# Inverse stage: the left-over rows of tiles 3 and 4 go through a DRAM stack of their own

## Chip, cores and metric

The kernel runs on one core of one Trainium2 chip. The metric is the device time of one launch in microseconds (us). Before the change it is 672.01 us (median of 3 runs, 671.79 to 672.07).

## What is computed

The input x has 2048 rows of 640 numbers in float32. A spectral layer is added to it and then a bilinear gated layer, each behind a layer norm:

```python
X = rfft2(layernorm(x)) * (w_r + 1j * w_i)
h = x + irfft2(X, s=(2048, 640))
n = layernorm(h)
out = h + ((n @ w_gate) * (n @ w_up)) @ w_down
```

## The kernel before

**Stages.** The transforms are done as matrix products on TensorE (PE). A forward stage turns the 16 tiles of 128 rows into spectra, a middle stage of 16 groups g multiplies by the filter, an inverse stage takes the 16 tiles t back along the 640 axis and the 2048 axis and adds x, and then the gated layer runs over blocks of weights until the end. The change lies in the inverse stage, with the last steps of the middle stage ahead of it.

**The inverse stage.** The middle stage leaves its result in two SBUF tensors: qm holds four main chunks of 128 frequencies for each tile, and qr the left-over frequencies, as a rounded high part (partitions 0 to 63) and a low part (partitions 64 to 127), with one edge frequency kept apart. For each tile, id_mm(t) multiplies the main chunks (matmuls eo<-tab,qm 128x161) and then the left-over rows into the same PSUM pair eo, of which there are two. unfold(t) takes eo through ScalarE (ACT, s), VectorE (DVE, q) and GpSimd (POOL, yt) to a buffer yt; is1_mm(t) multiplies that by the second transform (y<-yt,tab); acc(t) adds the result to x. The loop at the stage's end runs, for step t, unfold(t+2), id_mm(t+3), is1_mm(t), so PE's order is id 0, id 1, id 2, id 3, y 0, id 4, y 1, id 5, y 2 and on.

**Two ways for the left-over rows.** Tiles 0 to 4 are plain: five matmuls eo<-xt,qr of 322 columns with qr as it lies. Tiles 5 to 15 are stacked: high, low and high rows of one quarter lie above each other in 99 partitions, and four matmuls of 162 columns do the work (operand xt or si, 99 partitions). To move rows to other partitions the kernel goes through DRAM. ispread(a, o) writes the rows of some tiles from qr to a DRAM tensor ifar in five DMAs: two of 33 rows, two of 32 rows (L707) and one small one for the edge rows (L710). istack(t, n) reads n tiles back in two DMAs: 66 partitions (L718, high and low) and 33 partitions (L719, high again), each of 4 quarters times n x 128 numbers. Every piece of a row is n x 512 bytes long, and there are 99 x 4 = 396 pieces whatever n is.

**The order around the change.** All these DMAs are issued by one engine, SyncE (SP), in program order, and they share its queue. load_direct issues the first weight load (raw<-in_wlast_dram), then what is in its argument mid, then two more weight loads (raw<-in_wgu_dram), and istack for tiles 9 to 11 comes behind them. In mid stood: write tiles 5 to 8, read tiles 5 to 8, write tiles 9 to 15. istack for tiles 12 to 15 is issued when id_mm(8) is. A read waits on SP until the writes of its own DRAM tensor have landed, and what is behind it on SP waits too. Completion is counted on eight semaphores that SP's DMAs use in turn, so that a DMA also waits for the one eight places ahead of it to have landed. The weights that the two raw loads bring are split by ACT (L657, wdir) and POOL (L658) in the steps after (aside), between the unfold steps.

The stack of tiles 5 to 8 lies in the buffer near (named xt in the profile), the one of tiles 9 to 11 in the home "dC" (named si), and the one of tiles 12 to 15 in near again.

Of the kernel before, what the change touches and what calls it, by code (L numbers as in the profile page):

```python
# [11 lines left out]
F32 = mybir.dt.float32  # L12
F32R = mybir.dt.float32r
# [3 lines left out]
P = 128  # L17
S, D, NF, FF = 2048, 640, 321, 1728
NT = S // P
# [6 lines left out]
RWHERE = ((1, 0), (0, 0), (1, 160), (0, 160))  # L26
RW = (160, 194, 162, 162)
PLAIN, MID = 5, 10
IPLAIN, IFAR = 5, 9
SUMS = 7  # L30
IPARTS = ((5, 4), (9, 3), (12, 4))
AGAIN = {0: (5, 3, "dC"), 1: (8, 2, "qt"), 4: (10, 3, 0), 7: (13, 3, 1)}
NR = 4
AHEAD = 5
# [15 lines left out]
def f32(ap):  # L50
    return ap.bitcast(F32)
# [29 lines left out]
def tile_spectral_glu(ctx: ExitStack, tc: tile.TileContext, x, wre, wim, wgu, wlast, wdown, wdlast,  # L81
                      cc, ci, fmain, frem, imain, irem, mm, out):
    nc = tc.nc
# [4 lines left out]
    far = ctx.enter_context(tc.tile_pool(name="far", bufs=1, space=bass.MemoryType.DRAM))  # L88
# [16 lines left out]
    def pair(tag):  # L105
        return pools["a" if tag == "eo" else "y"].tile([P, 2, 512], F32, tag=tag, name=tag, bufs=2)
# [13 lines left out]
    def mmx(o, l, r, start, stop):  # L120
        nc.tensor.matmul(o, l, r, start=start, stop=stop, skip_group_check=True)  # L121
# [14 lines left out]
    def home(tag, shape, name, dt=F32):  # L136
        return keep.tile(shape, dt, tag=tag, name=name)

    def cut(t, o, *shape):
        v = t[:, o:o + int(np.prod(shape))]  # L140
        names = [f"d{i}" for i in range(len(shape))]
        return v.rearrange(f"p ({' '.join(names)}) -> p {' '.join(names)}", **dict(zip(names[1:], shape[1:])))
# [279 lines left out]
    def parts(ps, main, rest):  # L422
        for k, (b, o, w, l, r) in enumerate(main):
            mmx(ps[b][:, o:o + w], l, r, k < 2, False)
        for k, (b, l, r) in enumerate(rest):
            mmx(ps[b][:, 0:NQ], l, r, False, k >= len(rest) - 2)
# [154 lines left out]
    for g in range(NG - 1):  # L581
# [4 lines left out]
        if g + 3 == NG:  # L586
# [3 lines left out]
            scrap, near = cut(flat, 2258, D), cut(flat, 2258 + D, 4, 4, P)  # L590
# [20 lines left out]
        elif g == 1:  # L611
            rest_low(MID, NG)
            qr = home("qr", [P, 2, NT, P], "qr", F32R)
# [37 lines left out]
    def split_in(key, w, src, raws, engine):  # L651
        W[key] = w
        his, los = [], []
        for i, r in enumerate(raws):
            a, b = 640 * i, 640 * i + 640
            nc.sync.dma_start(r, src[:, a:b])
            his.append(lambda r=r, a=a, b=b: act(w[:, 0, a:b], r, AF.Copy))  # L657
            los.append(lambda r=r, a=a, b=b: engine.tensor_tensor(w[:, 1, a:b], r, f32(w[:, 0, a:b]), op=OP.subtract))  # L658
        return his, los

    def load_direct(blk, raws, engine=nc.gpsimd, mid=()):
        w = home("wA" if blk == 0 else "wB", [P, 3840], "wdir", F32R)
        first = split_in(NC - 1, cut(w, 0, 2, 640), wlast, raws[:1], engine)
        for f in mid:
            f()
        return [first, split_in(NC - 2, cut(w, 1280, 2, 1280), wgu[NC - 2], raws[1:], engine)]
# [30 lines left out]
    PE_, PY, YT, Z = {}, {}, {}, {}  # L697

    SI = {}
    ifar = [(a, far.tile([2, 2, 2, 33, b - a, P], F32, name="ifar")) for a, b in ((IPLAIN, IFAR), (IFAR, NT))]  # L700

    def ispread(a, o):
        ts = slice(a, a + o.shape[4])
        for h in (1, 0):
            for l in range(2):
                r = 64 * l + 31 * h
                nc.sync.dma_start(o[:, h, l, 1 - h:33].rearrange("b r t n -> r b t n"),  # L707
                                  f32(qr[r:r + 32 + h, :, ts]))
        e = f32(qr[0:65:64, 1, ts])
        nc.sync.dma_start(o[:, 0, :, 0].rearrange("b l t n -> l b (t n)"),  # L710
                          bass.AP(tensor=e.tensor, offset=e.offset,
                                  ap=[list(e.ap[0]), [0, 2], [1, P * o.shape[4]]]))

    def istack(t, n):
        o = near[:, :, 0:n] if t != 9 else home("dC", [P, 4, 3, P], "si", F32R)
        a, i = ifar[t >= IFAR]
        src = i[:, :, :, :, t - a:t - a + n].rearrange("b h l r t n -> (l r) (b h) (t n)")
        nc.sync.dma_start(f32(o[0:66]).rearrange("p q t n -> p q (t n)"), src)  # L718
        nc.sync.dma_start(f32(o[66:99]).rearrange("p q t n -> p q (t n)"), src[0:33])  # L719
        for i in range(n):  # L720
            SI[t + i] = o[:, :, i]

    def id_mm(t):
        ps = PE_[t] = pair("eo")
        main = [(b, o, 161, qm[:, c, t], imt[:, c]) for c, (b, o) in enumerate(((0, 0), (1, 0), (0, 161), (1, 161)))]
        if t not in SI:
            parts((ps[:, 0], ps[:, 1]), main,
                  [(b, qr[:, k, t], irt[:, c]) for c, b, k in ((0, 0, 0), (2, 0, 0), (1, 1, 1), (3, 0, 1), (4, 1, 1))])
            return
        parts((ps[:, 0], ps[:, 1]), main, [])  # L730
        for q, (b, h) in enumerate(((0, 0), (0, 1), (1, 0), (1, 1))):
            mmx(ps[:, b, 160 * h:160 * h + 162], SI[t][0:99, q], sirt[0:99, q], False, h == 1)
        if t == 8:
            istack(*IPARTS[2])

    def unfold(t, side, turns=(), extra=()):
        ps = PE_[t]
# [149 lines left out]
    for ts in (range(3), range(3, 6), range(6, 8)):  # L887
        n, t0 = len(ts), ts[-1] + 1
# [10 lines left out]

    tside[NT - 1] = []  # L900
    raw0 = home("dA", [P, 3, D], "raw0")
    jobs = load_direct(0, [raw0[:, i] for i in range(3)], mid=(
        lambda: ispread(*ifar[0]), lambda: istack(*IPARTS[0]), lambda: ispread(*ifar[1])))
    istack(*IPARTS[1])
    for i, (h, l) in enumerate((h, l) for hs, ls in jobs for h, l in zip(hs, ls)):
        aside[2 + i] += [h, l]
    id_mm(0)
    id_mm(1)
    unfold(0, [])
    id_mm(2)  # L910
    unfold(1, [])

# [640 lines left out]
```

## Time and profile before

| what | value |
|---|---|
| runs | 672.01 us (671.79 to 672.07) |
| the profiled execution, time | 672.12 us |
| its span | 670.3 us |
| PE busy | 661.2 us, 3695 matmuls |
| DVE, ACT, POOL busy | 468.7, 321.6, 393.3 us |
| inverse stage, first matmul of id_mm(0) | at 107.16 us |
| first matmul of the gated layer | at 151.5 us |

The span runs from the first to the last instruction of the program, and the time has 1.8 us around it. A matmul in float32 counts twice on PE (x8 in the trace for the four main matmuls of a tile), one in the rounded type fp32r once. Starts are given in us from the span's start. SPq is the queue side of SP; its time is the issue of a DMA, not the transfer.

### The profile page before, as it was taken

Reading aid. Unit: us, or ns where it says so; the run is one execution under the profiler, and the core shown is the slowest. Engines: PE = TensorE matmul, PEld = TensorE weight load, DVE = VectorE, ACT = ScalarE, POOL = GpSimd, SP = SyncE. Lnnn points to the kernel's source line nnn. Section 1 sums busy time; section 2 is a strip of 40 time slices with the busy share of each in tenths; the row PEclk is TensorE's granted clock in tenths of the full one; section 3 lists DMA queues with packets and bytes.
Section 4 is the critical chain, followed back from the end, with each engine's and each line's share of the span. In section 5 each row is a group of like instructions: output and inputs, shape, how many; then the busy total and the mean of one; then the engine's idle time right before and its main releaser. Section 6 shows DMA issues by size and latency. Waiting matters only on the chain.

```text
span 670.3 us, 10240 instructions
## 1 busy us (share of the span) xinstructions
PE 661.2 (99%) x3695; PEld 588.2 (88%) x3695; DVE 468.7 (70%) x952; ACT 321.6 (48%) x622; POOL 393.3 (59%) x377
## 2 busy tenths in 40 slices
PE   7999999999999999999999999999999999999997
PEld 7999988887888888888888899888888888888887
DVE  6969996788767767594857567754757485757644
ACT  6977774585525244453626146634434251624220
POOL 3101124750297977968696445188786869697610
PEclk9999999999999999999999999999999999999999
DMA  8639875502212120042332467212002121212004
GB/s 318 227 113 280 246 245 151 165 2 80 78 40 80 39 79 23 31 106 60 98 79 83 94 133 260 78 42 75 11 36 76 40 79 40 79 40 80 1 0 157
DMA packets 48953, 66.12 MB, mean 99 GB/s; under 512 B 24082, under 2 KB 30670, under 8 KB 48774
## 3 DMA queue, kind: packets, MB, share of 16 engines
q1 hardware_dynamic: 48246, 62.91, 30.4%
q0 software_dynamic: 288, 2.16, 0.8%
q8 instruction: 29, 0.48, 0.3%
q10 hardware_dynamic: 368, 0.39, 0.3%
q14 instruction: 22, 0.18, 0.1%
HBM read 54.61 MB, written 10.84 MB: 98 GB/s over the span
## 4 chain that ended last, share of the span: by engine, by line
PE 94%; ACT 2%; DVE 2%; DMA 1%; issue 0%; DVEq 0%
PE e L121 50%; PE d L121 26%; PE eo L121 4%; PE y L121 2%; PE re L121 2%; PE u L476 2%; PE im L121 2%; PE im L528 2%; PE im L270 2%; PE ir L528 1%; DMA x<-in_x_dram 1%; ACT s L296 1%; ACT fold L212 0%; ACT fold L211 0%; PE y L794 0%; ACT bits L285 0%
## 5 line engine op out<-in xcount | busy, mean ns | idle before, releaser
L121 PE MATMUL e<-xt,wst 128*128 128x512 f32 x864 | 211.1, 390 | 0.0
L121 PEld LDWEIGHTS e<-xt,wst 128*128 128x128 f32 x864 | 160.7, 188 | 31.7
L1073 DVE TENSOR_TENSOR x<-d,x 128x320 f32<-128x320 f32 x280 | 120.3, 482 | 41.2 <-PE d L121 37.1
L121 PE MATMUL d<-wd,ht 128*128 128x320 f32 x832 | 142.1, 309 | 0.0
L121 PEld LDWEIGHTS d<-wd,ht 128*128 128x128 f32 x832 | 129.6, 188 | 5.1
L987 POOL TENSOR_TENSOR wst<-raw,wst 128x1024 fp32r<-128x1024 f32 x23 | 55.5, 2412 | 69.9 <-ACT wst L986 69.9
L121 PE MATMUL e<-t,wst 128*128 128x512 f32 x360 | 94.0, 391 | 0.0
L121 PEld LDWEIGHTS e<-t,wst 128*128 128x128 f32 x360 | 66.7, 188 | 13.0
L121 PE MATMUL d<-wt,ht 128*128 128x320 f32 x360 | 68.9, 309 | 0.0
L1003 POOL TENSOR_TENSOR wst<-raw,wst 128x896 fp32r<-128x896 f32 (+1 forms) x46 | 65.1, 1438 | 0.2 <-ACT wst L998 0.2
L121 PEld LDWEIGHTS d<-wt,ht 128*128 128x128 f32 x360 | 57.3, 188 | 0.8
L1089 ACT ACTIVATE ht<-e 128x512 fp32r<-128x512 f32 x44 | 26.4, 599 | 49.6 <-DVE e L1151 24.0
L998 ACT ACTIVATE wst<-raw 128x896 fp32r<-128x896 f32 (+1 forms) x48 | 30.1, 676 | 30.8 <-POOL raw L992 30.1
L1147 DVE TENSOR_TENSOR e<-e,h 128x512 f32<-128x512 f32 x24 | 16.8, 698 | 39.8 <-ACT wst L998 18.9
L1048 DVE TENSOR_TENSOR x<-d,x 128x320 f32<-128x320 f32 x62 | 27.5, 484 | 22.2 <-PE d L121 22.2
L121 PE MATMUL e<-xt,wdir 128*128 128x512 f32 x180 | 42.2, 392 | 0.0
L679 ACT ACTIVATE wd<-draw 128x320 fp32r<-128x320 f32 (+1 forms) x30 | 15.7, 561 | 55.1 <-POOL draw L689 52.3
L1127 ACT ACTIVATE h<-e 128x512 f32<-128x512 f32 x24 | 14.3, 596 | 56.7 <-PE e L121 56.7
L121 PEld LDWEIGHTS e<-xt,wdir 128*128 128x128 f32 x180 | 33.3, 188 | 7.8 <-ACT xt L804 0.5
L1092 DVE TENSOR_TENSOR ht<-e,ht 128x512 fp32r<-128x512 f32 x54 | 36.9, 685 | 1.6 <-ACT ht L1089 1.3
L1144 ACT ACTIVATE h<-e 128x512 f32<-128x512 f32 x24 | 14.3, 597 | 46.7 <-PE e L121 46.7
L658 POOL TENSOR_TENSOR wd<-draw,wd 128x640 fp32r<-128x640 f32 x8 | 12.5, 1577 | 40.9 <-ACT wd L657 40.9
(236 smaller groups left out, 1188.9 us busy)
## 6 DMA issues: line engine op xcount, KB each, us to landing
raw<-in_wgu_dram SPq DMA_DIRECT2D x24, 640.0 KB
draw<-in_wdown_dram SPq DMA_DIRECT2D x24, 320.0 KB
wts<-in_wre_dram SPq DMA_DIRECT2D x16, 322.0 KB
x<-in_x_dram SPq DMA_DIRECT2D x15, 320.5 KB
out_dram<-x SPq DMA_DIRECT2D x15, 320.0 KB
bits<-in_mm_dram SPq DMA_DIRECT2D x32, 128.0 KB
wts<-in_wim_dram SPq DMA_DIRECT2D x9, 322.0 KB
zfar<-zr SPq DMA_DIRECT2D x32, 80.0 KB
```

The source lines that it names most:

```text
L121: nc.tensor.matmul(o, l, r, start=start, stop=stop, skip_group_check=True)
L528: nc.tensor.matmul(out, y[:, h, a:b], inv(g, h), start=n == 0, stop=n == len(ys) - 1)
L679: act(o[:, 0, a:a + n], src, AF.Copy)
L987: ptt(wa[:, 1], stage[:, 0:1024], f32(wa[:, 0]), op=OP.subtract)
L998: act(ws[:, 0, o:o + b - a], stage[:, a:b], AF.Copy)
L1003: ptt(ws[:, 1, o:o + b - a], stage[:, a:b], f32(ws[:, 0, o:o + b - a]), op=OP.subtract)
L1048: tt(xv, ps[b][:, 0:320], xv, op=OP.add)
L1073: tt(xv, o, xv, op=OP.add)
L1089: act(hop[:, a, 0], src, AF.Copy)
L1092: engine.tensor_tensor(hop[:, a, 1], src, f32(hop[:, a, 0]), op=OP.subtract)
L1127: act(h0, oa, AF.Copy)
L1147: tt(ob, ob, h1, op=OP.add)
```

## The change

Tiles 3 and 4 are stacked as well, with a DRAM tensor of their own. IFAR now lists three ranges of tiles (3 and 4; 5 to 8; 9 to 15), and IPARTS has a read of two tiles ahead of the others. ispread no longer issues its five DMAs at once but returns them as a list, and mid puts them in this order: the five writes of tiles 3 and 4, three of the five writes of tiles 5 to 8, the read of tiles 3 and 4, the other two writes of tiles 5 to 8, the read of tiles 5 to 8, the five writes of tiles 9 to 15. The two weight loads and the read of tiles 9 to 11 follow as before. The new stack lies in the home "dC", which the stack of tiles 9 to 11 takes over when id_mm(4) has read it.

```diff
--- before.py
+++ after.py
@@ -26,9 +26,9 @@
 RWHERE = ((1, 0), (0, 0), (1, 160), (0, 160))
 RW = (160, 194, 162, 162)
 PLAIN, MID = 5, 10
-IPLAIN, IFAR = 5, 9
+IFAR = ((3, 5), (5, 9), (9, NT))
 SUMS = 7
-IPARTS = ((5, 4), (9, 3), (12, 4))
+IPARTS = ((3, 2), (5, 4), (9, 3), (12, 4))
 AGAIN = {0: (5, 3, "dC"), 1: (8, 2, "qt"), 4: (10, 3, 0), 7: (13, 3, 1)}
 NR = 4
 AHEAD = 5
@@ -697,23 +697,26 @@
     PE_, PY, YT, Z = {}, {}, {}, {}
 
     SI = {}
-    ifar = [(a, far.tile([2, 2, 2, 33, b - a, P], F32, name="ifar")) for a, b in ((IPLAIN, IFAR), (IFAR, NT))]
+    ifar = [(a, far.tile([2, 2, 2, 33, b - a, P], F32, name="ifar")) for a, b in IFAR]
 
     def ispread(a, o):
         ts = slice(a, a + o.shape[4])
-        for h in (1, 0):
-            for l in range(2):
-                r = 64 * l + 31 * h
-                nc.sync.dma_start(o[:, h, l, 1 - h:33].rearrange("b r t n -> r b t n"),
-                                  f32(qr[r:r + 32 + h, :, ts]))
-        e = f32(qr[0:65:64, 1, ts])
-        nc.sync.dma_start(o[:, 0, :, 0].rearrange("b l t n -> l b (t n)"),
-                          bass.AP(tensor=e.tensor, offset=e.offset,
-                                  ap=[list(e.ap[0]), [0, 2], [1, P * o.shape[4]]]))
+
+        def rows_of(h, l):
+            r = 64 * l + 31 * h
+            nc.sync.dma_start(o[:, h, l, 1 - h:33].rearrange("b r t n -> r b t n"), f32(qr[r:r + 32 + h, :, ts]))
+
+        def edge_rows():
+            e = f32(qr[0:65:64, 1, ts])
+            nc.sync.dma_start(o[:, 0, :, 0].rearrange("b l t n -> l b (t n)"),
+                              bass.AP(tensor=e.tensor, offset=e.offset,
+                                      ap=[list(e.ap[0]), [0, 2], [1, P * o.shape[4]]]))
+
+        return [lambda h=h, l=l: rows_of(h, l) for h in (1, 0) for l in range(2)] + [edge_rows]
 
     def istack(t, n):
-        o = near[:, :, 0:n] if t != 9 else home("dC", [P, 4, 3, P], "si", F32R)
-        a, i = ifar[t >= IFAR]
+        o = near[:, :, 0:n] if t in (5, 12) else home("dC", [P, 4, n, P], "si", F32R)
+        a, i = [f for f in ifar if f[0] <= t][-1]
         src = i[:, :, :, :, t - a:t - a + n].rearrange("b h l r t n -> (l r) (b h) (t n)")
         nc.sync.dma_start(f32(o[0:66]).rearrange("p q t n -> p q (t n)"), src)
         nc.sync.dma_start(f32(o[66:99]).rearrange("p q t n -> p q (t n)"), src[0:33])
@@ -731,7 +734,7 @@
         for q, (b, h) in enumerate(((0, 0), (0, 1), (1, 0), (1, 1))):
             mmx(ps[:, b, 160 * h:160 * h + 162], SI[t][0:99, q], sirt[0:99, q], False, h == 1)
         if t == 8:
-            istack(*IPARTS[2])
+            istack(*IPARTS[3])
 
     def unfold(t, side, turns=(), extra=()):
         ps = PE_[t]
@@ -899,9 +902,10 @@
 
     tside[NT - 1] = []
     raw0 = home("dA", [P, 3, D], "raw0")
+    first, second, third = (ispread(*f) for f in ifar)
     jobs = load_direct(0, [raw0[:, i] for i in range(3)], mid=(
-        lambda: ispread(*ifar[0]), lambda: istack(*IPARTS[0]), lambda: ispread(*ifar[1])))
-    istack(*IPARTS[1])
+        *first, *second[:3], lambda: istack(*IPARTS[0]), *second[3:], lambda: istack(*IPARTS[1]), *third))
+    istack(*IPARTS[2])
     for i, (h, l) in enumerate((h, l) for hs, ls in jobs for h, l in zip(hs, ls)):
         aside[2 + i] += [h, l]
     id_mm(0)
```

On SP's queue, from the first left-over rows on, stood before (ifar<-qr are writes, xt<-ifar and si<-ifar reads; 512 numbers are four tiles, 896 seven, 384 three):

```order
L707 DMA ifar<-qr 33x2x512 x2
L707 DMA ifar<-qr 32x2x512 x2
L710 DMA ifar<-qr 2x2x512
L718 DMA xt<-ifar 66x4x512
L719 DMA xt<-ifar 33x4x512
L707 DMA ifar<-qr 33x2x896 x2
L707 DMA ifar<-qr 32x2x896 x2
L710 DMA ifar<-qr 2x2x896
L656 DMA raw_1298<-in_wgu_dram 128x640 x2
```

The read of tiles 5 to 8 was the sixth and seventh DMA of this list. The same place now (256 numbers are two tiles; the functions lie some lines further down, so L707, L711, L721 and L722 are the old L707, L710, L718 and L719):

```order
L707 DMA ifar<-qr 33x2x256 x2
L707 DMA ifar<-qr 32x2x256 x2
L711 DMA ifar<-qr 2x2x256
L707 DMA ifar<-qr 33x2x512 x2
L707 DMA ifar<-qr 32x2x512
L721 DMA si<-ifar 66x4x256
L722 DMA si<-ifar 33x4x256
L707 DMA ifar<-qr 32x2x512
L711 DMA ifar<-qr 2x2x512
L721 DMA xt<-ifar 66x4x512
L722 DMA xt<-ifar 33x4x512
L707 DMA ifar<-qr 33x2x896 x2
```

The new read of two tiles is the ninth and tenth DMA, and the read of tiles 5 to 8 has moved from the sixth place to the thirteenth; the remaining writes, the two weight loads and the read of tiles 9 to 11 follow behind it.

On PE, the difference at tiles 3 and 4 (eo<-tab,qm is a tile's main part, y<-yt,tab a second transform; the names in brackets are what the instruction waits for, DMAHW a DMA of SP):

```order
 L121 MATMUL eo<-tab,qm 128x161 x3
-L121 MATMUL eo<-xt,qr 128x322 x5
+L121 MATMUL eo<-xt,si 128x162 [waits DMAHW7_49,DMAHW0_49]
+L121 MATMUL eo<-xt,si 128x162 x3
 L121 MATMUL y<-yt,tab 128x320 [waits DMAHW2_49,Pool_49]
 L121 MATMUL y<-yt,tab 128x320
 L121 MATMUL eo<-tab,qm 128x161 [waits DVE_49,Activation_49]
 L121 MATMUL eo<-tab,qm 128x161 x3
-L121 MATMUL eo<-xt,qr 128x322 x5
+L121 MATMUL eo<-xt,si 128x162 x4
```

In each of the two tiles five matmuls of 322 columns have become four of 162, and the first of tile 3 waits for the two DMAs of the new read. Nothing else has moved on PE, nor on DVE, ACT or POOL.

## The prediction

> **What bounds the kernel now.** I read the page first, then the windows, then PE's timeline around the inverse stage, then SP's. The page gives the span and PE's share, and the clock that PE was granted in 40 slices:
>
> ```profile
> span 670.3 us, 10240 instructions
> PE 661.2 (99%) x3695; PEld 588.2 (88%) x3695; DVE 468.7 (70%) x952; ACT 321.6 (48%) x622; POOL 393.3 (59%) x377
> PEclk9999999999999999999999999999999999999999
> ```
>
> One window from the first tiles of the inverse stage nearly to the end (its length, then PE's busy time):
>
> ```profile
> 107.63:654.00 546.37, 546.37 (x2882) 1.00 0.24 71
> ```
>
> PE has no idle time in these 546.37 us. PE works in order, so a microsecond that PE loses or saves at tile 3 moves everything after it by a microsecond, unless something that doesn't hang on PE comes late. The change touches PE's work here (start, length, what):
>
> ```profile
> 112.79 1.26 PE L121 MATMUL eo<-tab,qm 128*128 128x161 f32 x8
> 113.78 1.01 PE L121 MATMUL eo<-xt,qr 128*128 128x322 f32 x5
> 114.63 1.24 PE L121 MATMUL y<-yt,tab 128*128 128x320 f32 x4
> ...
> 116.70 1.01 PE L121 MATMUL eo<-xt,qr 128*128 128x322 f32 x5
> ...
> 119.62 0.68 PE L121 MATMUL eo<-xt 99*128 99x162 f32 x4
> ```
>
> These are tile 3 (main at 112.79, left-over rows at 113.78), tile 4's left-over rows at 116.70, and at 119.62 the first stacked matmuls, those of tile 5. So PE asks for a stack of tile 5 at 119.62 now, and would ask for one of tile 3 at 113.78. When can the stacks be there? SP's issues, from the first left-over rows on:
>
> ```profile
> 106.76 2.19 SPq L707 DMA_DIRECT2D ifar<-qr  x4
> 109.00 0.58 SPq L710 DMA_DIRECT2D ifar<-qr  x1
> 111.06 0.30 SPq L718 DMA_DIRECT2D xt<-ifar  x1
> 111.41 0.39 SPq L719 DMA_DIRECT2D xt<-ifar  x1
> 111.85 2.18 SPq L707 DMA_DIRECT2D ifar<-qr  x4
> 114.06 0.51 SPq L710 DMA_DIRECT2D ifar<-qr  x1
> 114.61 3.07 SPq L656 DMA_DIRECT2D raw<-in_wgu_dram  x2
> 120.69 0.32 SPq L718 DMA_DIRECT2D si<-ifar  x1
> 121.05 0.39 SPq L719 DMA_DIRECT2D si<-ifar  x1
> 128.20 0.28 SPq L718 DMA_DIRECT2D xt<-ifar  x1
> ```
>
> The writes start at 106.76, when qr is ready, and take until 109.58 to issue. The read of tiles 5 to 8 starts at 111.06, when they have landed, 1.48 us later. It must be there at 119.62, and PE doesn't wait: the round trip through DRAM is hidden behind the five plain tiles, and it is this cover that the change shortens.
>
> **Term 1, the matmuls: 0.66 us less.** The chain of waits merges a tile's main part and left-over rows into one piece:
>
> ```profile
> 115.87 1.84 PE eo L121 x13
> ...
> 118.79 1.51 PE eo L121 x12
> ```
>
> A plain tile (x13, tile 4) costs 1.84 us and a stacked one (x12, tile 5) 1.51. Two tiles save 2 x 0.33 = 0.66 us, all on PE's path.
>
> **Term 2, when the small read is issued.** The five writes of tiles 3 and 4 have as many pieces as those of tiles 5 to 8 had, each half as long, and begin when qr is ready, so I leave their issue at 106.76 to 109.58. Three writes of tiles 5 to 8 come next; at 2.18 / 4 = 0.55 us each they are issued by 111.2. By then the first five have landed (111.06 before, with longer rows). The small read is issued at 111.2.
>
> **Term 3, how long it takes.** No read of two tiles stands alone in the trace. The nearest rows are the read of three tiles, issued at 120.69, and the last one of four, issued at 128.20. The traffic of the DMA engines after them, in slices of 0.15 us from 120.6 and of 0.2 us from 128:
>
> ```profile
> DMA  8662203983252677777877677676421000000000
> GB/s 324 256 273 103 102 34 75 113 72 61 61 102 102 236 266 266 276 266 236 195 143 164 154 215 205 236 256 205 113 51 21 0 0 0 0 0 0 0 0 0
> ```
>
> ```profile
> DMA  0000048924357786868677686776320000000000
> GB/s 0 0 0 0 0 61 102 102 92 102 82 205 276 287 266 164 195 143 195 143 205 215 174 174 143 195 205 154 92 62 20 0 0 0 0 0 0 0 0 0
> ```
>
> The first six slices of the upper pair are the end of the weights. Three tiles are read by 125.25 (31 slices), 4.56 us after the issue, and four by 134.2, 6.0 us after it. Between the last traffic and the release lies more, as the writes show (slices of 0.3 us from 106.6):
>
> ```profile
> GB/s 0 0 0 205 178 123 198 164 198 239 287 185 48 7 0 0 0 7 123 41 150 171 157 266 266 169 193 224 157 159 210 229 239 304 297 364 352 348 309 364
> ```
>
> Their traffic ends in the slice up to 110.8, and SP goes on at 111.06. I add 0.5: 5.05 us for three tiles and 6.5 for four. Going on along that line gives 5.05 - 1.45 = 3.6 for two. But each read has the same 396 pieces, and each begins with a slow microsecond (34 to 113 GB/s) whatever their length, so the line need not hold. I take the middle of 3.6 and 5.05, 4.3: the small stack is there at 111.2 + 4.3 = 115.5. PE wants it at 113.78 and waits 1.7 us.
>
> Here a rule of the Trainium skill would come out otherwise. Its page "DMA: Bandwidth & Descriptors", section "Anatomy of one DMA — SWDGE (gpsimd) path", gives a DMA 2.0 us and its bytes over 436 GB/s; for 396 pieces of 1 KB that is an estimate of 2.9 us. The rule is fitted on the other descriptor path, and for this queue the trace disagrees: by it four tiles would take 3.9 us, and their traffic alone lasted 6.0. By the rule the sum would be about 671.8 us.
>
> **Term 4, the read of tiles 5 to 8 moves behind the small one.** Two of its writes are now issued after the small read, and transfers queue: the writes issued from 111.85 on, behind the reads of tiles 5 to 8, hadn't landed until SP went on at 120.69, while the first five, with nothing ahead, needed 1.48. So the last two land after the small stack. For them I take 0.7 us, two of five writes of 1.5 us with SP's release (bounds 0.3 and 1.1). Then the read of tiles 5 to 8 is issued at 116.2 rather than 111.06, 5.1 us later, and needs 6.5 us: there at 122.7. Its bounds come from the row of SP's waits and the issue that ended one:
>
> ```profile
> SPq L656 <- DMA xt<-ifar: 0.6, 1, 0.6
> ```
>
> ```profile
> 116.26 1.43 SPq L656 DMA_DIRECT2D raw<-in_wgu_dram  x1
> ```
>
> A weight load waited for the first, longer half of the read until 116.26, 5.2 us after that half was issued; the shorter half follows. With other transfers about or not, I bound the whole by 6.3 and 6.7.
>
> **The sum.** PE now would reach tile 5's left-over rows at 119.62 - 0.66 + 1.7 = 120.7, and waits for them until 122.7, another 2.0 us. Against 119.62 that is 3.1 us late (1.7 + 2.0 - 0.66, rounded), and nothing after it gives time back, by the window above. The profiled execution took 672.12 us, so 675.2; the median of the runs before is 0.11 below it, less than the unknowns here.
>
> **What is queued behind.** The rows that need what comes after the read of tiles 5 to 8, in order of time:
>
> ```profile
> 121.35 0.74 ACT L657 ACTIVATE wdir<-raw 128x640 fp32r<-128x640 f32 x1 [0.53 <-DMA raw<-in_wgu_dram]
> ...
> 123.01 0.44 ACT L741 ACTIVATE s<-eo 128x322 f32<-128x322 f32 x1 [0.92 <-PE eo L121]
> ...
> 124.91 0.48 DVE L749 TENSOR_TENSOR q<-eo,s 128x322 f32<-128x322 f32 x1
> ...
> 130.12 0.68 PE L121 MATMUL eo<-xt,si 99*128 99x162 f32 x4
> ```
>
> The writes of tiles 9 to 15 and the weights follow the read of tiles 5 to 8 at the same distance as before, so all of them come 5.1 us later while PE is 3.1 late: their cover shrinks by 2.0. The read of tiles 9 to 11 is issued 120.69 - 111.06 = 9.63 us after that of tiles 5 to 8, at 125.8, and is there at 130.9; PE wants it at 130.12 + 3.1 = 133.2 (last row). The weights are closer. ACT already waits 0.53 us for the first of them. It would get it at 121.35 + 5.1 = 126.5 and be free at 127.2, where tile 6's s wants it at 123.01 + 3.1 = 126.1: 1.1 us late. DVE uses that s at 124.91, 1.46 us after its end, so this is hidden, narrowly, and I cost it at nothing. Were it later than 1.46, tile 6's PSUM would come free late and PE would wait a third time. "dC" costs nothing: id_mm(4) ends before 125.8.
>
> **The rivals.** Two rows for them: PE's longest wait before the change (total, times, longest), and the left-over rows of tile 6:
>
> ```profile
> PE im L270 <- DVE bits L287: 2.2, 2, 1.5
> ```
>
> ```profile
> 122.24 0.69 PE L121 MATMUL eo<-xt 99*128 99x162 f32 x4
> ```
>
> - *Only tile 3 waits.* If the read of tiles 5 to 8 is there by 120.7, the price is 1.7 - 0.66 = 1.0 us: 673.2. It needs that read in 4.5 us, against 6.0 of traffic in the row; or a small read at the low end, 3.6, with a smaller stall. Chance 0.09.
> - *No wait, not slower.* Short pieces are so quick that the small stack is there by 113.78, 2.6 us after its issue, and tile 5's by 119.0, PE's new time for it. Then the 0.66 us are all: 671.5. It decides at 2.6 us for the small read, and needs the one of tiles 5 to 8 in 4.5 as well; against it stands that three tiles, half as many bytes again, took 4.56 of traffic. Chance 0.04.
> - *The weights hold ACT.* If they come over 1.46 us late for tile 6's s, PE waits again; at 2 us more this is 677.2. For it speaks that the cover was already gone by 0.53 us before the change. Chance 0.08.
> - *The clock falls in the waits.* PE idles twice for about 2 us. Before, its longest idle time is 1.5 us, and the page shows the full clock in every slice. If the granted clock halved after the second wait for one tile's period, 2.62 us (119.62 to 122.24), PE would lose that much more: 677.8. Chance 0.04. The Trainium skill's "TensorE: Matmul & The Clock Gate", Part 1 on the HAM clock gate, puts the drop at an idle window of about 3.4 us, which neither of my waits fills; no run here shows a drop.
>
> **How the numbers follow.** The forecast, both stacks late, has 0.75. Its low end: the small read takes 3.6, the rest 0.3, the big read 6.3, from 111.1: 121.3, or 1.7 us over 119.62, 673.8. Its high end: 111.3 + 5.05 + 1.1 + 6.7 = 124.15, or 4.5 over, 676.6. The range takes in part of the rivals on both sides: 673.2 to 677.5, which leaves out the case of no wait (0.04), half of tile 3 alone (0.05), most of the fall of the clock (0.03), half of the case of the weights (0.04) and the tails of the forecast (0.03). About 0.2%, 1.34 us, is what a measurement of this kernel can tell from no change. Faster by more than that is out of reach, since the whole gain is 0.66: 0.01. Within it lie no wait, tile 3 alone, and a small lower tail of the forecast: 0.14. Slower: 0.85.
>
> **What would show it.** Right: PE idle for about 1.7 us ahead of tile 3's stacked matmuls and about 2.0 ahead of tile 5's, both released by DMA si<-ifar or xt<-ifar; SP issuing the read of tiles 3 and 4 near 111.2 and that of tiles 5 to 8 near 116.2; tiles 3 and 4 at 1.51 us of work each; no PE idle time from tile 6 to 650 us. Wrong: tile 5's stack there without a wait, the small read done in under 3.6 us, or new idle time further down, ahead of tile 8 or 9.

## The result and the profile after

The changed kernel takes 676.5 us (median of 6 runs, 675.86 to 677.03) against 672.04 (671.79 to 672.6): a ratio of 1.0064, 95% interval 1.0053 to 1.0074. It is slower by 4.5 us; 675.2 was forecast. The profiled execution took 676.01 us with a span of 674.2, 3.9 us over that of before.

```profile
span 674.2 us, 10249 instructions
PE 663.1 (98%) x3693; PEld 589.3 (87%) x3693; DVE 468.6 (70%) x952; ACT 321.8 (48%) x622; POOL 393.7 (58%) x377
```

PE's timeline at the same tiles (the inverse stage begins at 107.33 here, 107.16 before, so 0.17 is taken off when the two are compared):

```profile
112.94 1.26 PE L121 MATMUL eo<-tab,qm 128*128 128x161 f32 x8
116.02 0.77 PE L121 MATMUL eo<-xt,si 99*128 99x162 f32 x4 [1.81 <-DMA si<-ifar]
116.59 2.41 PE L121 MATMUL y<-yt,tab 128*128 128x320 f32 x4
118.80 1.79 PE L121 MATMUL eo<-tab,qm 128*128 128x161 f32 x8
120.32 0.68 PE L121 MATMUL eo<-xt,si 99*128 99x162 f32 x4
120.84 1.28 PE L121 MATMUL y<-yt,tab 128*128 128x320 f32 x4
121.95 1.26 PE L121 MATMUL eo<-tab,qm 128*128 128x161 f32 x8
123.81 0.65 PE L121 MATMUL eo<-xt 99*128 99x162 f32 x4 [0.60 <-DMA xt<-ifar]
```

Tile 3's left-over rows start at 116.02 instead of 113.78, behind an idle time that the small read ends. Tile 5's start at 123.81 instead of 119.62, behind one that the read of tiles 5 to 8 ends. Between them two steps are slow: y took 1.24 us before and takes 2.41, the main part of tile 4 1.79 instead of 1.26. The windows show why (PE's busy time, then the granted clock):

```profile
116.00:120.00 4.00, 3.98 (x13) 0.57 0.43 95
120.00:124.00 4.00, 3.40 (x23) 1.00 1.01 272
124.00:654.00 530.00, 530.00 (x2780) 1.00 0.23 69
```

A mean of 0.57 over 4 us is 3.4 us at half clock, right behind the first wait. From 124 on PE is as full as before, so what is late at tile 5 stays late to the end. SP's issues, and the chain of waits that ends at tile 5:

```profile
111.28 0.28 SPq L721 DMA_DIRECT2D si<-ifar  x1
111.61 0.44 SPq L722 DMA_DIRECT2D si<-ifar  x1
112.09 0.35 SPq L707 DMA_DIRECT2D ifar<-qr  x1
112.49 0.52 SPq L711 DMA_DIRECT2D ifar<-qr  x1
116.54 0.29 SPq L721 DMA_DIRECT2D xt<-ifar  x1
```

```profile
112.49 4.00 DMA ifar<-qr
...
116.88 6.80 DMA xt<-ifar
```

The last little write of tiles 5 to 8, issued at 112.49, lands at 116.49, behind the small read. Only then does SP issue the read of tiles 5 to 8, and its second half lands at 123.68. The chain holds no work of PE in these 11 us: in this execution transfers alone set the time of tile 5.

### The profile page after: what moved, and what is told of

Same layout as the page of the kernel before. It is cut to its first block, busy times and chain, and to the rows that moved or that the text cites. A ratio compares the mean times of both kernels' runs of the same rounds, so it can differ in the third digit from the quotient of the medians.

```text
span 674.2 us, 10249 instructions
## 1 busy us (share of the span) xinstructions
PE 663.1 (98%) x3693; PEld 589.3 (87%) x3693; DVE 468.6 (70%) x952; ACT 321.8 (48%) x622; POOL 393.7 (58%) x377
## 4 chain that ended last, share of the span: by engine, by line
PE 92%; DMA 3%; DVE 2%; ACT 2%; issue 0%; SPq 0%; POOL 0%; DVEq 0%; POOLq 0%
PE e L121 50%; PE d L121 26%; PE eo L121 3%; PE re L121 2%; PE y L121 2%; PE u L476 2%; PE im L121 2%; PE im L528 2%; PE im L270 2%; DMA xt<-ifar 1%; DMA ifar<-qr 1%; PE ir L528 1%; DMA x<-in_x_dram 1%; ACT s L296 1%; ACT fold L212 0%; ACT fold L211 0%
```

## The experiments

All edits are to the changed kernel, and code fences show only the lines concerned. The kernel before was run along with them in two groups. It took 671.99 us (671.8 to 672.33) beside "All DMAs", "One set of writes", "The same with PE kept busy" and "The changed kernel with PE kept busy", and 672.24 us (671.71 to 673.05) beside the other four. Every run also has the mean of its granted clock: 3.4 us at half clock lower it by 3.4 x 0.5 / 674 = 0.0025, so 0.999 and 1.0 stand for no such stretch and 0.997 for one. The PE and SP rows of an experiment are from one execution. The stage began at slightly different times in them; where stacks of different runs are compared, the times are set to the start of before (107.16).

After the first result there were two theories and a rival to both. Theory: the stack of tiles 5 to 8 is late because of what stands ahead of its read on SP's queue, above all SP's second wait for writes. Rival "first wait": tile 3's wait, with the halved clock behind it, is what is paid. Rival "volume": the added bytes alone make the stack that late, in any order.

### All DMAs, no use of the small stack

```diff
-        if t not in SI:
+        if t not in SI or t < 5:
```

> All DMAs of the changed kernel, but tiles 3 and 4 computed in the plain way from qr, so that nobody waits for the small stack. Theory: tile 5's stack lands as late as in the changed kernel, PE waits 3.9 us ahead of tile 5, and the time is 4.0 us over the kernel before, or 5.7 if the clock halves behind that wait with nothing to cover it. Rival (the wait of tile 3 is the cause, and tile 5's only follows from it): no wait left, within 0.3 us of the kernel before.

Measured: 677.22 us (674.67 to 678.57), ratio 1.0074 (1.0061 to 1.0088). PE, and SP's issue of the read of tiles 5 to 8:

```profile
118.38 1.26 PE L121 MATMUL eo<-tab,qm 128*128 128x161 f32 x8
122.52 0.65 PE L121 MATMUL eo<-xt 99*128 99x162 f32 x4 [2.88 <-DMA xt<-ifar]
```

```profile
115.85 0.29 SPq L721 DMA_DIRECT2D xt<-ifar  x1
```

```profile
122.00:127.00 5.00, 4.48 (x18) 0.66 0.80 284
```

Nobody waits for the small stack, and the kernel is as slow as ever. Rival "first wait" falls: the tile 5 stack's lateness is not a consequence of tile 3's. The clock halves behind this wait too (0.66 over 5 us is 3.4 us at half), and here nothing covers it: 2.88 us of wait and 1.7 of clock make 4.6, as the profiled run has (676.76 against 672.12), and the one run at clock 1.0 took 674.67. The wait is 1.0 us below the 3.9 that I gave. The stage began at 106.91, so the stack of tile 5 is there at 122.77, 0.9 earlier than in the changed kernel (123.64) though its DMAs are the same. One execution's landing is therefore uncertain by nearly 1 us.

### The small read left out, its writes kept

```diff
-        *first, *second[:3], lambda: istack(*IPARTS[0]), *second[3:], lambda: istack(*IPARTS[1]), *third))
+        *first, *second, lambda: istack(*IPARTS[1]), *third))
```

> The changed kernel without the small read: tiles 3 and 4 are written to DRAM but not read back, and computed in the plain way. Theory (what delays tile 5's stack is a chain on one queue, the larger part of it the small read, which the last writes of tiles 5 to 8 and SP's wait for them stand behind): the read of tiles 5 to 8 is issued near 113.6 us, 2.9 us earlier than in the changed kernel, its stack is there at 120.3 to 120.7, and PE waits 0.7 to 1.1 us: 0.7 to 1.1 us over the kernel before. Rival (the five added writes alone push it that far): as late as in the run with all DMAs and no use of them, 4 us over and more.

Measured: 672.53 us (672.03 to 672.88), ratio 1.0003 (0.9994 to 1.0012), no difference that can be told. SP and PE:

```profile
113.13 0.30 SPq L721 DMA_DIRECT2D xt<-ifar  x1
```

```profile
120.42 0.65 PE L121 MATMUL eo<-xt 99*128 99x162 f32 x4 [0.59 <-DMA xt<-ifar]
```

The five added writes push the read of tiles 5 to 8 from 111.06 to 113.13, 2.1 us, and most of that was slack: PE idles 0.59, a little under my band, and so is the time, 0.3 over the kernel before. The small read with its consequences pushes it on to 116.37 (116.54 less 0.17). Writes alone are not the cause: rival "volume" falls as far as the five added writes go.

### One set of writes for tiles 3 to 8

```diff
-IFAR = ((3, 5), (5, 9), (9, NT))
+IFAR = ((3, 9), (9, NT))
-    first, second, third = (ispread(*f) for f in ifar)
+    first, second = (ispread(*f) for f in ifar)
-        *first, *second[:3], lambda: istack(*IPARTS[0]), *second[3:], lambda: istack(*IPARTS[1]), *third))
+        *first, lambda: istack(*IPARTS[0]), lambda: istack(*IPARTS[1]), *second))
```

> One set of five writes for tiles 3 to 8, then the read of tiles 3 and 4 and right behind it that of tiles 5 to 8, so only one wait of SP for writes is left. Theory (the second trip through DRAM sets the end: the read of tiles 5 to 8 is held back until writes land that queue behind the small read): tile 3 waits somewhat longer than in the changed kernel, 2.0 to 2.6 us, tile 5 no longer waits, and the time is 2.5 to 3.9 us over the kernel before, the upper end if the clock halves for 3.4 us behind the wait (1.7 us of it then shows). Rival (volume: the same bytes cross the same queue, so tile 5's stack is as late as before): it is there 4.0 us late again, and the time is 4.0 to 4.5 over.

Measured: 675.19 us (674.33 to 677.92), ratio 1.0055 (1.0039 to 1.0072); the profiled run took 675.93. SP and PE:

```profile
112.17 0.30 SPq L721 DMA_DIRECT2D si<-ifar  x1
...
112.95 0.37 SPq L721 DMA_DIRECT2D xt<-ifar  x1
```

```profile
116.65 0.65 PE L121 MATMUL eo<-xt,si 99*128 99x162 f32 x4 [2.59 <-DMA si<-ifar]
...
118.87 2.32 PE L121 MATMUL eo<-tab,qm 128*128 128x161 f32 x8
...
123.54 0.69 PE L121 MATMUL eo<-xt 99*128 99x162 f32 x4
```

Tile 5 no longer waits, as the theory said. By itself that does not decide against volume, since PE came to tile 5 only at 123.54 and a stack landing at 123.5 would have been in time; the next run decides it. That 123.54 is hardly earlier than 123.81 is the halved clock, which is not covered here: from tile 3's to tile 5's left-over rows PE takes 6.89 us (116.65 to 123.54) where the same work takes 119.62 - 113.78 - 0.66 = 5.18. The 1.7 us between them are the clock's.

### The same with PE kept busy in tile 3's wait

```diff
+        for k in range(9 if t == 3 else 0):
+            mmx(ps[:, 0, 330:491], qm[:, k % 4, t], imt[:, k % 4], False, False)
```

The added matmuls stand ahead of the stacked ones and write columns of the PSUM pair that nobody reads.

> The single set of writes with nine such matmuls (2.2 us) in tile 3's wait. Theory: here nothing covers the clock any more, so that keeping PE busy takes 1.7 us off against the single set of writes alone: 1.4 to 2.0 us over the kernel before, tile 3's wait less 0.66 us of saved matmuls. Rival volume: tile 5 waits in its place and the time is 4.0 to 4.5 over. If the clock doesn't halve in the single set of writes either, both are equal.

Measured: 674.34 us (673.92 to 674.8), ratio 1.0034 (1.0022 to 1.0046). Its window over the same tiles has the full clock, and tile 5 comes 1.76 us earlier, without a wait:

```profile
116.00:121.00 5.00, 4.94 (x30) 1.00 0.97 215
```

```profile
121.78 0.68 PE L121 MATMUL eo<-xt 99*128 99x162 f32 x4
```

So with one set of writes the stack of tile 5 is there by 121.78: in this order the same bytes do not make it 4 us late, and volume falls for this order. Against 675.93 of the profiled run without the added matmuls, this one took 674.34. So the clock is worth 1.6 us where nothing covers it. The runs without the added matmuls say the same: three at a clock of 0.999 to 1.0 took 674.33 to 674.46, the profiled one at 0.997 took 675.93, and two at 0.995 took 677.54 and 677.92. Against the kernel before, 2.35 us remain, above the 1.4 to 2.0 that I gave.

### The changed kernel with PE kept busy in tile 3's wait

The edit is the last one with 7 in place of 9, on the changed kernel.

> The changed kernel with seven more matmuls of 161 columns (1.74 us, into unused columns of the PSUM tile, read by nobody) between tile 3's main part and its stacked part, so that PE is busy in its wait and the clock has no reason to halve. Theory (the landing of tile 5's stack sets the end): PE comes to tile 5 about 1.7 us earlier, waits the longer there, and the time stays within 0.3 us of the changed kernel, 676.2 to 676.8. Rival (the halved clock behind tile 3's wait is what is paid): 1.7 us less, 674.8.

Measured: 675.7 us (675.14 to 677.46), ratio 1.0065 (1.0052 to 1.0078).

```profile
115.97 0.68 PE L121 MATMUL eo<-xt,si 99*128 99x162 f32 x4
...
120.22 1.26 PE L121 MATMUL eo<-tab,qm 128*128 128x161 f32 x8
123.07 0.65 PE L121 MATMUL eo<-xt 99*128 99x162 f32 x4 [1.58 <-DMA xt<-ifar]
```

With the clock kept up PE comes to tile 5 sooner and waits longer, 1.58 us against 0.60. So in the profiled execution of the changed kernel most of what the clock took lay inside the second wait. The median is 0.5 below the band that I gave, and 0.9 above the rival's 674.8. In the profile the difference is the stack's: it came 0.8 us earlier than in the changed kernel (the stage begins at 107.42 there, so 123.07 less 0.26, against 123.81 less 0.17). SP issued that read 0.5 us earlier, at 116.10 less 0.26 against 116.54 less 0.17, while the clock of the changed kernel fell only near 116.5, so the fall did not delay that issue. How much of the 0.8 us between the two medians is the clock in other executions is not shown.

### PE kept busy in both waits

```diff
+        for k in range({3: 7, 5: 6}.get(t, 0)):
+            mmx(ps[:, 0, 330:491], qm[:, k % 4, t], imt[:, k % 4], False, False)
```

> The changed kernel with matmuls of 161 columns that nobody reads in both waits: seven ahead of tile 3's stacked part, six (1.5 us) ahead of tile 5's. Theory: the spread of the times of the run with filled first wait alone (675.1 to 677.5) is the clock behind the second wait; with both filled the times stay within 674.9 to 675.9, the landing of tile 5's stack. Rival (the spread is that of the DMAs): it is as wide as before, with times over 677 among five or six.

Measured: 675.62 us (675.24 to 677.29; the five are 675.24, 675.48, 675.62, 676.3 and 677.29), ratio 1.0058 (1.0044 to 1.0071). PE has no idle time in the whole window that served before:

```profile
107.63:654.00 546.37, 546.37 (x2889) 1.00 0.24 72
```

My theory on the spread holds in part. With the first wait alone filled, the two runs over 677 (677.42 and 677.46) have a clock of 0.997 and the three others 1.0, so the clock did fall in the high ones. But with both waits filled 677.29 came at 0.999 and 676.3 at 1.0, above my band. That this rest is the transfers' own spread fits, but no run over 677 was profiled, so this stays open.

### All writes ahead of the small read

```diff
-        *first, *second[:3], lambda: istack(*IPARTS[0]), *second[3:], lambda: istack(*IPARTS[1]), *third))
+        *first, *second, lambda: istack(*IPARTS[0]), lambda: istack(*IPARTS[1]), *third))
```

> All five writes of tiles 5 to 8 ahead of the small read, so that SP doesn't wait for writes between the two reads. Theory: the small read is issued about 1 us later and tile 3 waits 2.7 to 3.3 us; the read of tiles 5 to 8 follows it at once, is there near 122, and tile 5 doesn't wait. Time as with one set of writes for tiles 3 to 8: 2.0 to 2.6 us over the kernel before if the clock stays up, 1.7 us more for each 3.4 us at half clock, so 2.0 to 6. Rival (volume): tile 5's stack at 123.5 as in the changed kernel, and a second wait there.

Measured: 675.06 us (674.54 to 675.49), ratio 1.004 (1.0028 to 1.0053). SP's two reads, PE, and PE's windows:

```profile
111.92 0.35 SPq L721 DMA_DIRECT2D si<-ifar  x1
...
113.16 0.28 SPq L721 DMA_DIRECT2D xt<-ifar  x1
```

```profile
116.37 0.65 PE L121 MATMUL eo<-xt,si 99*128 99x162 f32 x4 [2.37 <-DMA si<-ifar]
...
122.45 0.65 PE L121 MATMUL eo<-xt 99*128 99x162 f32 x4 [0.60 <-DMA xt<-ifar]
```

```profile
116.00:122.00 6.00, 5.49 (x32) 1.00 0.89 239
```

The read of tiles 5 to 8 is issued at 113.16, no later than without any small read (113.13), but PE gets its stack at 122.45 instead of 120.42. Those 2.0 us are the queue: the small read's pieces go first. Set to the same start (107.11 here) the stack is there at 122.50, 1.1 us earlier than in the changed kernel's profile (123.64), but only 0.3 earlier than in the two other executions with that kernel's DMAs in which PE waited for it (122.77 and 122.81). So SP's second wait is worth 0.3 to 1.1 us, though it has the read issued 3.2 us later (116.37 against 113.16 with 0.05 added). The small read on the queue had the larger share, and I had given the second wait too much. The clock stayed up in this execution, behind a wait of 2.37 us, so PE reached tile 5 soon enough to wait there after all; I had expected none. In two of the other four runs the clock was 0.997.

### The small read by itself

```diff
+            if t == 8:
+                istack(*IPARTS[3])
             return
-        *first, *second[:3], lambda: istack(*IPARTS[0]), *second[3:], lambda: istack(*IPARTS[1]), *third))
+        *first, lambda: istack(*IPARTS[0]), *third))
```

> Tiles 3 and 4 stacked, tiles 5 to 8 plain, neither written nor read; so the small read has its own five writes ahead and nothing else. It tells what the small read takes by itself: 4.5 to 4.7 us from issue to PE's release if that is its own price (my theory now), 3.6 if the three writes between had slowed it. With its own price tile 3 waits 1.7 to 1.9 us, tiles 3 and 4 save 0.66, and four plain tiles cost 1.32: 2.4 to 2.6 us over the kernel before with the clock up, 1.7 more for each 3.4 us at half clock.

Measured: 673.89 us (673.24 to 674.36), ratio 1.0024 (1.0014 to 1.0034).

```profile
111.25 0.30 SPq L721 DMA_DIRECT2D si<-ifar  x1
```

```profile
115.37 0.65 PE L121 MATMUL eo<-xt,si 99*128 99x162 f32 x4 [1.16 <-DMA si<-ifar]
```

From issue to PE's release the small read takes 4.12 us with nothing of tiles 5 to 8 ahead of it, and 4.74 in the changed kernel (111.28 to 116.02). Neither of my two values: its own price is above 3.6, and in the changed kernel, with three writes queued ahead, it is 0.6 higher. (What is queued behind differs too: the seven tiles' writes here, two writes there.) PE idles 1.16 us, so with 0.66 saved and four plain tiles at 0.33 more each, 1.8 us were to come, and 1.65 came, less than the 2.4 to 2.6 that I gave because the read took less.

## Why the prediction was right, and where it was short

- **What bounds the kernel.** Right. PE is full from 124 to 654 us, and the time follows tile 5: 4.0 us late there (123.81 - 0.17 - 119.62), 3.9 in the span. The medians differ by 4.5; the profiled run of the changed kernel is 0.5 below its median, and that half microsecond has no row. Both waits came, released by the DMAs named, but not at the forecast sizes: 1.81 and 0.60 against 1.7 and 2.0. That 3.1 came near 4.0 is in part luck: the clock's 1.7 us and the second wait overlap.
- **Term 1, 0.66 us of matmuls.** Right in size: a tile takes 1.51 us stacked (tile 4 at full clock, 117.60 to 119.11 with the first wait filled), and the arithmetic of the small read alone comes out with it. It was lost among the waits.
- **Term 2, the small read issued at 111.2.** 111.28.
- **Term 3, 4.3 us for it and tile 3 late by 1.7.** Mis-sized: 4.74 us, and tile 3 was 2.1 late (116.02 - 0.17 - 113.78), 0.3 more than the idle time of 1.81 since the main part's modelled end lies behind 113.78. By itself it takes 4.12; the 0.6 more goes with the three writes queued ahead, which I had costed at nothing, but it rests on one execution each and wasn't taken apart further. The two rows that I took as ends, 3.6 and 5.05, held it.
- **Term 4, the rest of the writes 0.7 and the big read 6.5.** The read was issued 0.5 us after PE's release for tile 3. From its issue to PE's release it took 7.27 us, over the upper bound of 6.7; in the other runs 6.67 (all DMAs, no use), 6.97 (filled first wait) and 7.29 (no small read). I took the price from the last read of the stage, behind which nothing is issued for long; this one has seven tiles of writes and the weights right behind it. That these slow it was not tried by itself.
- **The sum.** 3.1 forecast, 4.0 in the profile: 0.4 more is the small read and 0.8 the big one, less 0.3 for the issue and the writes between. In order of the queue, for the profiled execution: five added writes 2.1, the small read ahead on the queue 2.0, SP's second wait 1.1 (0.3 by the other two executions), together 5.3 us of later landing, of which some 1.3 had been slack (118.35, an estimate, is 111.06 plus the 7.29 of the run without a small read; PE asked at 119.62).
- **The rule of 2.0 us and bytes over 436 GB/s.** The Trainium skill's page "DMA: Bandwidth & Descriptors", section "Anatomy of one DMA — SWDGE (gpsimd) path", gives a fit from which 2.9 us was estimated for the small read. The traces disagree for this queue: 4.12 at its shortest.
- **The clock.** I gave its fall a chance of 0.04 and a price at the second wait. In the profiled execution it fell, at the first, and five of the six runs have a mean clock of 0.997. In the profile its 1.7 us didn't show, since PE would have waited for tile 5's stack anyway; the run with one set of writes shows the price where that cover is gone. My chance was far too low; that it hardly changed the sum there was the second wait's doing. The medians with filled waits are 0.8 to 0.9 lower (675.7 and 675.62), so in other executions some of it may have been paid.
- **The weights on ACT.** Late as forecast, and hidden: ACT waited longer for them than before, 1.99 us against 0.53, and no idle time of PE followed.

```profile
126.98 0.74 ACT L657 ACTIVATE wdir<-raw 128x640 fp32r<-128x640 f32 x1 [1.99 <-DMA raw<-in_wgu_dram]
```

## What to carry to other kernels

Before work is moved to a form that needs a round trip through memory, set the time at which its consumer asks against the whole trip, with everything that shares the queue: here 0.33 us a tile was bought with a trip whose last hop alone took 4 us, due 7 us after the data was ready. A small urgent transfer put ahead of a large one delayed the large one by its time on the queue, 2.0 us here, and by 0.3 to 1.1 more where the issuing engine then waited for something that had queued behind it. And when a wait of the busy engine is priced, ask what it does to the clock, and whether a later wait would hide that.

## What the runs showed of the hardware

- The granted clock halved for 3.4 us behind PE waits of 1.81, 2.59 and 2.88 us (the changed kernel, one set of writes, all DMAs without use), and not behind waits of 2.37 (all writes first), 1.58 and 1.16. By half-microsecond windows it fell only after PE had resumed, 0.4, 1.0 and 0.6 us later. So the length of a wait alone doesn't decide, and the same kernel can go either way: of the six runs of the changed kernel one had the full clock throughout, of the six with one set of writes three. The Trainium skill's "TensorE: Matmul & The Clock Gate", Part 1 on the HAM clock gate, puts the drop after an idle window of about 3.4 us; the 3.4 us of the slow stretch agree with that length, the wait needed for it does not, and the measurements decide.
- A stack read has the same 396 pieces whatever its tiles, and its price grows less than its bytes: 4.12 us for two tiles alone, 6.67 to 7.29 for four. The read of two tiles also begins slowly: in the run with the small read by itself, the queue's traffic stays at 53 GB/s or less until 112.75, 1.5 us after the issue.
- With both reads in the changed kernel's order the times spread more: 675.14 to 677.46 with the first wait filled, against 671.8 to 672.33 of the kernel before run along with it. The clock is part of it, as told above. It is no rule for every wait on such a read: without the small read the times were 672.03 to 672.88, with it alone 673.24 to 674.36.
